# Attention with mixed heads on one Trainium2 core: a head's scores moved in one transfer, and a new order of even and odd steps

## The chip, the cores and the metric

The kernel runs on one core of a Trainium2 chip. The metric is the device time of one execution in microseconds (us). It is the median of several runs. A profile of one further execution shows what each engine and each transfer did.

The engines are named as in the profile: PE (TensorE, matmuls) with PEld (its loads of weights), DVE (VectorE), ACT (ScalarE), POOL (GpSimd) and SP (SyncE). SP does no arithmetic: its queue (SPq) issues nearly all transfers, which 16 DMA engines carry out.

## The reference

Attention whose heads are mixed before and after the softmax, then a feed-forward part with squared ReLU, then a feed-forward part in which each token goes to one of eight experts:

```python
# q, k, v: [4, 12, 448, 64]
scores = scale * q @ k.T                                  # per batch and head: [448, 448]
scores = np.einsum('bhij,hg->bgij', scores, w_pre)        # mix heads
attn = np.exp(scores - max(scores))
attn = attn / (sum(attn) + 1e-9)
attn = np.einsum('bhij,hg->bgij', attn, w_post)           # mix heads again
x = attn @ v                                              # then both feed-forward parts
```

The change is in attention alone.

## The kernel before

Attention works in chunks. A chunk is ten rows of queries with all twelve heads, 120 rows in all, laid over the partitions, so that mixing heads is a matmul over partitions. A batch has 45 chunks (`NCH`), there are four batches, and a step of the main loop in `attention` (variable `g`) finishes one chunk.

*Scores.* `scores(b, t, h)` computes 120 rows (90 for `t` = 3) of one head's scores on PE (L256, L257), copies them from PSUM to a buffer `s` (L260, mostly on ACT; four buffers, `sp`), and sends them with two transfers from SP (L267) into the tile `tt[b, t]`. The transfers put row group `i` of head `h` on partition `12 i + h`: five groups (`HI`) from partition 0 on, the other five from partition 64 on, 60 partitions (`KH`) each. A tile `tt[b, t]` thus gathers twelve heads, and serves twelve chunks (nine for `t` = 3). There are three such tiles in turn.

*Mixing before the softmax.* `pre(b, c)` makes two chunks at a time: four matmuls (L279) of 60 rows by 64 columns of weights `kpre`, each over 448 columns; then the negated maxima on DVE (L292), then two exponentials on ACT (L301) with their sums. `norm` (L310, L311, L313) takes the reciprocal on DVE and scales the second mixing's weights with it on POOL (`kp`).

*Mixing after it.* `post` has four matmuls with `kp` (L323) and moves the result from PSUM to `at` (L331), by ACT for the chunks in `EVAC` and by DVE for the others. `pv` multiplies nine chunks at a time by the values (L344), in two halves; `pv_lo` and `pv_out` split the result in two parts and send it to DRAM (L375).

*Preparation.* `prep` transposes queries and keys of the next batch (L200) and splits them into a high and a low part (L214 on ACT, L233 on DVE); it is a generator in two parts, and a key's high part is copied to the other partitions by SP (L235). `load` (L175) and `load_v` (L243) bring the inputs. For the first batch some of this is done by POOL (L218, L228).

The order is written by hand. `on(g, f, ...)` puts a call into step `g`, with lists such as `PREP` (when a preparation begins) and `EVAC`. Each step has this order:

```python
norm(g + 1)
exp2 = pre(g + 2)      # if that chunk's number is even; exp2 is its second exponential
rest of the step       # scores, prep, pv_lo, pv_out, loads
exp2()
post(g)
pv                     # where one is due
```

Of the kernel before, what the change touches and what calls it, by code (L numbers as in the profile page):

```python
# [19 lines left out]
B, H, S, D = 4, 12, 448, 64  # L20
# [5 lines left out]
II = 10  # L26
NCH = 45
KP = II * H

HI = II // 2  # L30
KH = HI * H
TOKT = 112

TT = 128
# [69 lines left out]
def constants():  # L104

    cols = [n for c in range(NCH) for n in chunk_rows(c)]
    cols = np.array([n for i, n in enumerate(cols) if i not in DUPS])

    orig = np.zeros((128, 3, NTT))
    for t in range(NTT):  # L110
        row = t * TT + np.arange(TT)
        orig[:, 0, t] = (row + 1) // 32 * 32
        orig[:, 1, t] = (row + 1) % 32
        orig[:, 2, t] = row // S * S + cols[row % S]
    orig = orig.reshape(128, -1)
    ident = np.eye(128)
    mask = np.zeros((128, II))
    for i in range(2):
        mask[64 * i:64 * i + KH, HI * i:HI * i + HI] = np.repeat(np.eye(HI), H, axis=0)
    tri = np.triu(np.ones((128, 128)), 1)  # L120
    iota = np.tile(np.arange(128), (128, 1))
    below = np.tile(np.tril(np.ones((NE, NE)), -1).reshape(1, -1), (128, 1))
    im8 = iota[:, :NE] - NE
    return np.concatenate([ident, mask, orig, tri, iota, below, im8], 1).astype(np.float32)

F64_MIN = float(np.array([0x38000000], np.uint32).view(np.float32)[0])
F64_MAX = float(np.array([0x47EFFFFF], np.uint32).view(np.float32)[0])

C_ID, C_MASK, C_ORIG, C_TRI, C_IOTA, C_BELOW, C_IM8 = 0, 128, 138, 180, 308, 436, 500
NCONST = 508


def attention(tc, cst, q, k, v, w_pre, w_post, xscr, nb, tail=None):
    nc = tc.nc
    GC = 9
    NGR = NCH // GC

    def left(name, bufs=1):  # L140
        return Areas(tc, name, bufs)

    wp, at1, vp, xp, mp = left("wp"), left("at1"), left("vp"), left("xp"), left("mp", 3)
    tb, at0, tm, sp, ta = left("tb"), left("at0"), left("tm"), left("sp", 4), left("ta")

    ap_ = (at1, at0) if (NGR * nb - 1) % 2 == 0 else (at0, at1)
    tps = [(tb, ta, tm)[(k + 1 - 4 * nb) % 3] for k in range(3)]
# [10 lines left out]
    ident = cst[:TOKT, C_ID:C_ID + TOKT]  # L158
# [89 lines left out]
    tt = {}  # L248

    def scores(b, t, h):  # L250
        p, j = divmod(h, 2)
        zq = zt[b, p, "q"][0][:, j]
        zkh, zkl = zt[b, p, "k"][0][:, j], zt[b, p, "k"][1]
        n0, m = (120 * t, 120) if t < 3 else (358, 90)
        pq = qk.tile([128, 512], F32, tag="qk", name="pq")
        nc.tensor.matmul(pq[:m, :S], zq[:, n0:n0 + m], zkh, start=True, stop=False)  # L256
        nc.tensor.matmul(pq[:m, :S], zq[:, n0:n0 + m], zkl[:, j], start=False, stop=True)  # L257
        s = sp.tile([120, S], F32, tag="s", name="s")
        eng = nc.vector.tensor_copy if b == t == 0 and h % 3 == 2 else nc.scalar.copy
        eng(s[:m], pq[:m, :S])  # L260
        if h == 0:
            tt[b, t] = tps[(4 * b + t) % 3].tile([128, 12, S], F32, name="t")

        w = m // II
        for j in range(2):
            rows_h = tt[b, t][64 * j:64 * j + KH].rearrange("(i h) r s -> h i r s", h=H)[h]
            nc.sync.dma_start(out=rows_h[:, :w], in_=s[HI * w * j:HI * w * j + HI * w])  # L267

    st = {}

    def pre(b, c):

        t, r = divmod(c, 12)
        single = c == NCH - 1
        pms = [pre_.tile([128, 512], F32, name="pre") for _ in range(2)]
        for i, j in ((0, 0), (1, 1), (0, 1), (1, 0)):
            if single and i != j:
                continue
            nc.tensor.matmul(  # L279
                pms[i][64 * j:64 * j + 64, :S],  # L280
                kpre[64 * i:64 * i + KH],
                tt[b, t][64 * i:64 * i + KH, r if single else r + j],
                start=True,
                stop=True,
            )

        alls = slice(0, 128)
        parts = [(pms[i], halves[i], 0) for i in range(2)] if single else [(pms[i], alls, i) for i in range(2)]
        n = 1 if single else 2
        mxs = [mp.tile([128, 4], F32, tag="mx", bufs=6, name="mx") for _ in range(n)]  # L290
        for pm, q, i in parts:
            nc.vector.tensor_reduce(  # L292
                out=mxs[i][q, 0:1], in_=pm[q, :S], axis=AX.X, op=ALU.max, negate=True
            )
        es = [e_tile() for _ in range(n)]
        for i in range(n):
            st[b, c + i] = [es[i], mxs[i]]

        def exp(k):
            pm, q, i = parts[k]  # L300
            nc.scalar.activation(  # L301
                out=es[i][q], in_=pm[q, :S], func=AF.Exp, bias=mxs[i][q, 0:1], accum_out=mxs[i][q, 1:2]
            )

        exp(0)
        return lambda: exp(1)

    def norm(b, c):
# [97 lines left out]
    tmp = e_tile()  # L406
    wraw = tmp[:, :2 * H].rearrange("p (i h) -> p i h", i=2)
    nc.vector.memset(tmp[:, :2 * H], 0.0)
    for i, w in enumerate((w_pre, w_post)):
        for j in range(2):  # L410
            nc.sync.dma_start(
                out=wraw[64 * j:64 * j + KH, i, :],
                in_=w.rearrange("(o h) g -> o h g", o=1).to_broadcast([HI, H, H]),
            )
    live = [prep(0, *u) for u in units]
    for i in range(len(units) + 3):
        if i < len(units):
# [8 lines left out]
            if LEAD + i - 2 < len(units):  # L426
                load(0, *units[LEAD + i - 2])
    kpre, kpost = (wp.tile([128, n], F32, name=nm) for nm, n in (("kpre", 64), ("kpost", KP)))
    mask = cst[:, C_MASK:C_MASK + II]
    nc.gpsimd.memset(kpre, 0.0)  # L430

    def kron(out, i, q, cols):
        n = cols.stop - cols.start
        nc.gpsimd.tensor_tensor(
            out=out,
            in0=wraw[q, i, :].rearrange("p (h o) -> p h o", o=1).to_broadcast([q.stop - q.start, H, n]),
            in1=mask[q, cols].rearrange("p (o i) -> p o i", o=1).to_broadcast([q.stop - q.start, H, n]),
            op=ALU.mult,
        )

    for j in range(2):
        hq = halves[j]
        kron(kpre[hq, :KH].rearrange("p (i g) -> p g i", i=HI), 0, hq, slice(HI * j, HI * j + HI))
    kron(kpost.rearrange("p (g i) -> p g i", i=II), 1, slice(0, 128), slice(0, II))
    nc.gpsimd.tensor_scalar_mul(kpre, kpre, 1.0 / float(D) ** 0.5)
    chunks = [(b, c) for b in range(nb) for c in range(NCH)]
    at_step = {}
# [1 line left out]
    def on(g, f, *a):  # L449

        rank = 0 if f is go else 2 if f is begin else 1
        at_step.setdefault(g, []).append((rank, f, a))
# [14 lines left out]

    PREP = (14, 15, 17, 19, 20, 22, 24, 25, 27, 29, 31, 32)  # L470
    EVAC = range(15, 34, 3)
    for b in range(nb):
        o = b * NCH
        for h in range(H):
            if b == 0:
                on(-4 + 8 * h // 12, scores, 0, 1, h)
            on(o + (4 if b == 0 else 2) + 10 * h // 12, scores, b, 2, h)
            on(o + 12 + 10 * h // 12, scores, b, 3, h)
            if b + 1 < nb:
                on(o + 26 + 11 * h // 12, scores, b + 1, 0, h)  # L480
                on(o + 37 + 10 * h // 12, scores, b + 1, 1, h)
        for gr in range(NGR):
            end = o + GC * gr + GC
            first, gap = (2, 2) if gr < NGR - 1 and b < nb - 1 else (1, 1)
            if b == nb - 1 and gr == NGR - 1:
                first = 0
            for hf in range(2):
                for i, f in enumerate((pv, pv_lo)):
                    on(end + first + gap * hf + i, f, b, gr, hf)
            on(end + first + gap + 2, pv_out, b, gr)  # L490
        if b + 1 < nb:
            for i, u in enumerate(units):
                spread(o + PREP[i], 2, prep, b + 1, *u)
                on(o + (PREP[i - XB] + 1 if i >= XB else 8 + i), load, b + 1, *u)
        for i in range(4):
            on(o + 3 + 2 * i - 2 * (b == 0), load_v, b, i)

    n = len(chunks)
    last = max(list(at_step) + [n])
    for g in range(-4, last + 1):  # L500
        if 0 <= g + 1 < n:
            norm(*chunks[g + 1])
        exp2 = None
        if 0 <= g + 2 < n and chunks[g + 2][1] % 2 == 0:
            exp2 = pre(*chunks[g + 2])
        rest = [x[1:] for x in sorted(at_step.get(g, []), key=lambda x: x[0])]
        for f, a in rest:
            if f is not pv:
                f(*a)
        if exp2:  # L510
            exp2()
        if 0 <= g < n:
            post(*chunks[g])
        for f, a in rest:
            if f is pv:
                f(*a)
        rel = g - (nb - 1) * NCH
        if rel == 23:
            close(ta, sp, ld, zp, qk)
        if rel == 34:  # L520
            close(tm)
        if rel == 39:
            close(at0)
        if rel == 43:
            close(tb)
        if tail:
            tail(rel)
# [873 lines left out]
```

## Time and profile before

| | |
|---|---|
| time before, median of 3 runs | 1372.76 us (1372.42 to 1373.51) |
| profiled execution, its own time | 1374.09 us |
| its span, first to last instruction | 1372.2 us |
| PE busy | 1282.0 us, 93% of the span |
| DVE busy | 983.3 us, 72% |
| ACT busy | 746.3 us, 54% |
| POOL busy | 162.6 us, 12% |
| mean granted clock of TensorE | 0.978 |

Busy shares are means over stages of different kinds: attention fills the first part of the span, the feed-forward parts the rest. Register, branch and semaphore instructions and the issuing of transfers are not counted as busy. The granted clock is a share of full speed, and has two levels, 1.2 and 2.4 GHz.

### The profile page before, as it was taken

What the parts mean: (1) busy time and instruction counts of PE and PEld (TensorE: products, weight loads), DVE (VectorE), ACT (ScalarE), POOL (GpSimd) and SP (SyncE); (2) the same over time, 40 slices, a digit from 0 to 9 for tenths busy, and PEclk for the clock granted to TensorE, in tenths of its full rate; (3) what the DMA queues carried; (4) which work ended last, traced back from release to release, by engine and by line L of the source; (5) the groups of instructions that cost most, each with busy time, mean ns of one, the idle gap of its engine ahead of it and who ended that gap; (6) DMA issues with size and microseconds to landing.
All of it is one profiled execution on the core that took longest, in us unless ns stands there. A gap on an engine that the chain in (4) does not pass through costs nothing. (4 is left out here: it accounts for less than half of the span.)

```text
span 1372.2 us, 26014 instructions
## 1 busy us (share of the span) xinstructions
PE 1282.0 (93%) x9235; PEld 1116.3 (81%) x9235; DVE 983.3 (72%) x1965; ACT 746.3 (54%) x1469; POOL 162.6 (12%) x249
## 2 busy tenths in 40 slices
PE   6889988998899898999999999999998999999997
PEld 4556666766667676899999999999987899999996
DVE  5447655764676457767986899689647688898887
ACT  5456545654565366454332333333225588889886
POOL 3112221221122122000000000000000111111110
PEclk9899998999999899999999999999999999999999
DMA  5357445645564456756545555446475494556551
GB/s 155 128 150 151 115 132 154 147 118 134 150 142 129 138 120 226 232 184 249 212 189 226 193 227 225 193 176 254 157 263 191 149 361 164 169 179 249 162 179 39
DMA packets 157771, 243.86 MB, mean 178 GB/s; under 512 B 84323, under 2 KB 128707, under 8 KB 149956
## 3 DMA queue, kind: packets, MB, share of 16 engines
q1 hardware_dynamic: 154836, 229.54, 51.6%
q0 software_dynamic: 2800, 12.61, 2.6%
q8 instruction: 75, 1.23, 0.4%
q14 instruction: 60, 0.49, 0.1%
HBM read 236.48 MB, written 23.21 MB: 189 GB/s over the span
## 5 line engine op out<-in xcount | busy, mean ns | idle before, releaser
L323 PEld LDWEIGHTS post_post<-mp_kp,mp_e 128*112 128x112 f32 x1440 | 173.2, 180 | 22.3 <-POOL mp_kp L313 12.5
L323 PE MATMUL post_post<-mp_kp,mp_e 128*112 128x120 f32 x1440 | 181.9, 271 | 6.0 <-POOL mp_kp L313 5.3
L301 ACT ACTIVATE mp_e<-pre_pre,mp_mx 128x448 f32<-128x448 f32 (+1 forms) x184 | 117.1, 637 | 92.3 <-DVE mp_mx L292 91.4
L292 DVE TENSOR_REDUCE mp_mx<-pre_pre 128x1 f32<-128x448 f32 (+1 forms) x184 | 106.4, 618 | 74.0 <-PE pre_pre L279 73.6
L677 PE MATMUL hp_h<-m1x_xl,m1w_ih 128*128 128x384 f32 (+1 forms) x480 | 156.2, 325 | 2.7 <-DMA m1x_xl<-xscrl 2.7
L677 PE MATMUL hp_h<-m1x_xh,m1w_ih 128*128 128x384 f32 (+1 forms) x480 | 156.7, 326 | 0.5 <-DMA m1x_xh<-xscrh 0.5
L260 ACT COPY sp_s<-qk_qk 120x448 f32<-120x448 f32 (+1 forms) x188 | 98.3, 529 | 108.2 <-DMA tb_t<-sp_s 38.4
L686 ACT ACTIVATE m1g_r<-hp_h 128x384 f32<-128x384 f32 (+1 forms) x80 | 37.6, 470 | 218.5 <-PE hp_h L677 205.5
L313 POOL TENSOR_SCALAR mp_kp<-wp_kpost,mp_mx 128x120 f32<-128x120 f32 x180 | 106.3, 592 | 419.7 <-DVE mp_mx L311 355.5
L677 PE MATMUL hp_h<-m1x_xh,m1w_il 128*128 128x384 f32 (+1 forms) x480 | 155.9, 325 | 0.0
L1154 DVE TENSOR_TENSOR m2w_w2l<-m2r_r,m2w_w2h 128x768 fp32r<-128x768 f32 x130 | 116.2, 951 | 33.8 <-ACT m2w_w2h L1153 33.7
L331 DVE COPY at_at<-post_post 112x480 f32<-112x480 f32 x130 | 85.3, 656 | 50.9 <-PE post_post L323 50.1
L770 PE MATMUL acc_a<-m1w_oh,m1g_gl 128*128 128x384 f32 (+1 forms) x436 | 113.2, 341 | 4.1 <-DVE m1g_gl L689 3.9
L770 PE MATMUL acc_a<-m1w_ol,m1g_gh 128*128 128x384 f32 (+1 forms) x436 | 112.3, 339 | 0.0
L770 PE MATMUL acc_a<-m1w_oh,m1g_gh 128*128 128x384 f32 (+1 forms) x436 | 112.1, 338 | 0.0
L784 DVE TENSOR_TENSOR y_y<-acc_a,y_y 128x384 f32<-128x384 f32 x196 | 96.3, 552 | 11.0 <-PE acc_a L770 10.7
L256 PE MATMUL qk_qk<-zp_zk,zp_zq 128*120 128x448 f32 (+1 forms) x192 | 87.1, 453 | 15.5 <-DVE zp_zl L233 5.4
L256 PEld LDWEIGHTS qk_qk<-zp_zk,zp_zq 128*120 128x120 f32 (+1 forms) x192 | 35.0, 182 | 80.5 <-issue 51.5
L1153 ACT CAST m2w_w2h<-m2r_r 128x768 fp32r<-128x768 f32 x130 | 99.0, 841 | 0.3 <-PE m2p_a L1215 0.2
L344 PE MATMUL pv_pv<-at_at,vp_v 112*64 112x90 f32 x1872 | 86.5, 250 | 7.2 <-DMA vp_v<-in_v 6.6
L677 PEld LDWEIGHTS hp_h<-m1x_xl,m1w_ih 128*128 128x128 f32 x480 | 90.5, 189 | 3.2 <-DMA m1x_xl<-xscrl 3.2
L689 DVE TENSOR_TENSOR m1g_gl<-m1g_r,m1g_gh 128x384 fp32r<-128x384 f32 (+1 forms) x78 | 41.1, 528 | 72.2 <-ACT m1g_gh L688 72.2
(239 smaller groups left out, 2697.1 us busy)
## 6 DMA issues: line engine op xcount, KB each, us to landing
m2r_r<-in_moe_w SPq DMA_DIRECT2D x107, 512.0 KB
m2r_r<-in_moe_w SPq DMA_DIRECT2D x136, 384.0 KB
m1x_xh<-xscrh SPq DMA_DIRECT2D x29, 1152.0 KB
m1x_xl<-xscrl SPq DMA_DIRECT2D x29, 1152.0 KB
m1raw_rawi<-in_moe_w_in SPq DMA_DIRECT2D x16, 768.0 KB
m1raw_rawo<-in_moe_w_out SPq DMA_DIRECT2D x16, 768.0 KB
tb_t<-sp_s SPq DMA_DIRECT2D x96, 105.0 KB
ta_t<-sp_s SPq DMA_DIRECT2D x96, 105.0 KB
```

The source lines that it names most:

```text
L256: nc.tensor.matmul(pq[:m, :S], zq[:, n0:n0 + m], zkh, start=True, stop=False)
L260: eng(s[:m], pq[:m, :S])
L292: nc.vector.tensor_reduce(out=mxs[i][q, 0:1], in_=pm[q, :S], axis=AX.X, op=ALU.max, negate=True)
L301: nc.scalar.activation(out=es[i][q], in_=pm[q, :S], func=AF.Exp, bias=mxs[i][q, 0:1], accum_out=mxs[i][q, 1:2])
L313: nc.gpsimd.tensor_scalar_mul(kp, kpost, mx[:, 3:4])
L323: nc.tensor.matmul(po[:, r].rearrange("p g i -> p (g i)"), ev[:, r], kp, start=True, stop=True)
L344: nc.tensor.matmul(px[64 * o:64 * o + 64, p], vt[b][:, g, r], a[:, r, g].rearrange("p c i -> p (c i)"), start=(r == 0), stop=(r == 3),)
L677: nc.tensor.matmul(ph, w[:, k], x, start=(kt == 0 and i == 0), stop=(kt == KT - 1 and i == 2))
L770: nc.tensor.matmul(p, g[:, c], w[:, HM * h:HM * h + (m if h else HM)], start=(j == 0 and i == 0), stop=(j == GF - 1 and i == 2),)
L784: nc.vector.tensor_add(y, p, y)
L1153: nc.scalar.copy(wh, raw)
L1154: nc.vector.tensor_sub(wl, raw, wh.bitcast(F32))
```

## The change

1. A head's scores go in one transfer: ten row groups on partitions `LOW + 12 i + h`, that is 4 to 123, without a gap. The two mixing matmuls now take rows 0 to 63 and 64 to 123. The first four partitions are set to zero once in each of the three tiles, by POOL, and the mixing weights `kpre` are built over 128 partitions with a mask of their own.
2. Five buffers `s` in place of four.
3. In a step the second exponential of the pair before comes first, then the second parts of preparations, then `norm`, the rest, and only then `pre`, `post` and `pv`.
4. Preparations begin in even steps from 14 to 36 of a batch, scores have steps written out (`TILES`), mostly odd ones where preparations run, and `pv` comes in odd steps. `pre` is in even steps, as before.
5. ACT evicts the twelve even chunks from 14 to 36, in place of seven from 15 to 33.
6. The last chunk of a batch, which is a pair of halves, has both exponentials at once.

The core of the diff:

```diff
+LOW = 64 - KH
...
-    tb, at0, tm, sp, ta = left("tb"), left("at0"), left("tm"), left("sp", 4), left("ta")
+    tb, at0, tm, sp, ta = left("tb"), left("at0"), left("tm"), left("sp", 5), left("ta")
...
-        w = m // II
-        for j in range(2):
-            rows_h = tt[b, t][64 * j:64 * j + KH].rearrange("(i h) r s -> h i r s", h=H)[h]
-            nc.sync.dma_start(out=rows_h[:, :w], in_=s[HI * w * j:HI * w * j + HI * w])
+            if 4 * b + t < 3:
+                nc.gpsimd.memset(tt[b, t][:LOW], 0.0)
+
+        rows_h = tt[b, t][LOW:LOW + KP].rearrange("(i h) r s -> h i r s", h=H)[h]
+        nc.sync.dma_start(out=rows_h[:, :m // II], in_=s[:m])
...
-                kpre[64 * i:64 * i + KH],
-                tt[b, t][64 * i:64 * i + KH, r if single else r + j],
+                kpre[64 * i:LOW + KH + KH * i],
+                tt[b, t][64 * i:LOW + KH + KH * i, r if single else r + j],
...
-    PREP = (14, 15, 17, 19, 20, 22, 24, 25, 27, 29, 31, 32)
-    EVAC = range(15, 34, 3)
+    PREP = range(14, 38, 2)
+    EVAC = range(14, 38, 2)
+    TILES = (
+        (25, 25, 27, 27, 29, 31, 33, 33, 35, 37, 39, 39),
+        (35, 37, 38, 40, 41, 41, 42, 43, 43, 44, 45, 46),
+        (2, 3, 3, 4, 5, 6, 7, 8, 9, 10, 11, 12),
+        (13, 13, 15, 15, 17, 17, 19, 19, 21, 21, 23, 23),
+    )
...
-            on(o + (4 if b == 0 else 2) + 10 * h // 12, scores, b, 2, h)
-            on(o + 12 + 10 * h // 12, scores, b, 3, h)
+            on(o + (4 + 9 * h // 12 if b == 0 else TILES[2][h]), scores, b, 2, h)
+            on(o + TILES[3][h], scores, b, 3, h)
             if b + 1 < nb:
-                on(o + 26 + 11 * h // 12, scores, b + 1, 0, h)
-                on(o + 37 + 10 * h // 12, scores, b + 1, 1, h)
+                on(o + TILES[0][h], scores, b + 1, 0, h)
+                on(o + TILES[1][h], scores, b + 1, 1, h)
...
-            first, gap = (2, 2) if gr < NGR - 1 and b < nb - 1 else (1, 1)
+            first, gap = (2 - gr % 2 if gr < NGR - 1 else 1, 2) if b < nb - 1 else (1, 1)
...
+    exp2 = None
     for g in range(-4, last + 1):
+        todo = sorted(at_step.get(g, []), key=lambda x: x[0])
+        rest = [[x[1:] for x in todo if (x[0] == 0) == i] for i in (True, False)]
+        if exp2:
+            exp2()
+        exp2 = None
+        for f, a in rest[0]:
+            f(*a)
         if 0 <= g + 1 < n:
             norm(*chunks[g + 1])
-        exp2 = None
+        for f, a in rest[1]:
+            if f is not pv:
+                f(*a)
         if 0 <= g + 2 < n and chunks[g + 2][1] % 2 == 0:
             exp2 = pre(*chunks[g + 2])
...
-        if exp2:
-            exp2()
         if 0 <= g < n:
             post(*chunks[g])
-        for f, a in rest:
+        for f, a in rest[1]:
             if f is pv:
                 f(*a)
```

## Rows read from the trace of the kernel before

**Rows 1.** Busy time by stretch: stretch, length, engines' busy us (instructions), clock, DMA share, GB/s

```profile
173.80:305.90 132.10, 117.32 (x1167) 87.38 (x1165) 80.31 (x208) 72.36 (x182) 26.18 (x45) 0.95 0.54 137
...
196.60:229.60 33.00, 24.09 (x210) 17.22 (x209) 12.02 (x34) 13.52 (x33) 4.52 (x8) 0.79 0.50 141
229.60:282.10 52.50, 47.02 (x493) 35.34 (x492) 39.01 (x97) 35.73 (x88) 10.94 (x20) 1.00 0.62 144
...
328.70:361.20 32.50, 24.89 (x220) 18.17 (x219) 13.15 (x36) 13.45 (x34) 4.66 (x8) 0.84 0.53 144
...
459.00:486.00 27.00, 21.33 (x185) 15.26 (x184) 9.74 (x27) 9.79 (x25) 3.49 (x6) 0.81 0.37 118
...
44.40:97.00 52.60, 45.06 (x342) 31.51 (x341) 24.95 (x67) 24.63 (x62) 9.04 (x16) 0.94 0.46 137
```

**Rows 2.** Who waited for whom, 60 to 480 us: total us, times, longest us

```profile
ACT sp_s L260 <- DMA tm_t<-sp_s: 30.3, 17, 4.9
ACT sp_s L260 <- DMA tb_t<-sp_s: 30.0, 16, 5.9
...
ACT sp_s L260 <- DMA ta_t<-sp_s: 24.3, 16, 5.2
```

**Rows 3.** Timeline around 200 us: start, us, instruction, idle before it and its releaser

```profile
199.46 0.53 ACT L260 COPY sp_s<-qk_qk 120x448 f32<-120x448 f32 x1 [5.85 <-DMA tb_t<-sp_s]
...
200.67 0.19 PEld L279 LDWEIGHTS pre_pre<-tm_t,wp_kpre 60*64 60x64 f32 x2 [3.81 <-ACT mp_e L301]
```

**Rows 4.** Timeline of SP's queue, 176 to 230 us: start, us, issues

```profile
182.67 4.81 SPq L267 DMA_DIRECT2D tb_t<-sp_s  x6
...
189.52 2.89 SPq L375 DMA_DIRECT2D xscrh<-xp_xh  x1
...
218.55 10.50 SPq L267 DMA_DIRECT2D ta_t<-sp_s  x10
```

**Rows 5.** Issues by line: ns least/median/most, first and last start; then sizes

```profile
L267 SPq DMA_DIRECT2D ta_t<-sp_s x120: 712/727/2912, 33.1 to 443.5; - x120
...
L235 SPq DMA_DIRECT2D zp_zk<-zp_zk x36: 512/545/1859, 99.7 to 409.6; - x36
...
L175 SPq DMA_DIRECT2D ld_x<-in_q x18: 642/650/1702, 72.2 to 385.6; - x18
...
L375 SPq DMA_DIRECT2D xscrh<-xp_xh x28: 519/610/2892, 97.5 to 565.7; - x28
...
tb_t<-sp_s SPq DMA_DIRECT2D x96, 105.0 KB
```

**Rows 6.** Busy time while SP issues scores only (columns as in rows 1)

```profile
182.70:187.40 4.70, 4.70 (x69) 3.67 (x66) 2.49 (x8) 1.92 (x5) 0.79 (x2) 1.00 0.33 120
```

**Rows 7.** Timeline of one chain from mixing to the next weights

```profile
233.16 0.98 PE L279 MATMUL pre_pre<-tm_t,wp_kpre 60*64 60x448 f32 x8
...
234.19 1.16 DVE L292 TENSOR_REDUCE mp_mx<-pre_pre 128x1 f32<-128x448 f32 x2
...
234.85 0.63 ACT L301 ACTIVATE mp_e<-pre_pre,mp_mx 128x448 f32<-128x448 f32 x1 [1.26 <-DVE mp_mx L292]
...
235.38 1.26 DVE L233 TENSOR_TENSOR zp_zq<-qk_qk,zp_zq 64x448 fp32r<-64x448 f32 x2
...
236.67 0.15 DVE L310 TENSOR_SCALAR mp_mx<-mp_mx 128x1 f32<-128x1 f32 x1
...
237.29 0.58 POOL L313 TENSOR_SCALAR mp_kp<-wp_kpost,mp_mx 128x120 f32<-128x120 f32 x1 [2.26 <-DVE mp_mx L311]
```

**Rows 8.** Groups by line: busy us, mean ns of one, idle before

```profile
L331 DVE COPY at_at<-post_post 112x480 f32<-112x480 f32 x130 | 85.3, 656 | 50.9 <-PE post_post L323 50.1
...
L331 ACT COPY at_at<-post_post 112x480 f32<-112x480 f32 x50 | 27.9, 571 | 2.4 <-PE post_post L323 2.2
```

**Rows 9.** The first 40 us: POOL's zeroing, and the first mixing

```profile
L228 POOL MEMSET zp_zl<- x12: 464/466/467, 9.3 to 24.6; 64x448 f32 x12
...
37.01 2.55 PE L279 MATMUL pre_pre<-tb_t,wp_kpre 60*64 60x448 f32 x8 [5.31 <-DMA tb_t<-sp_s]
```

More of the change, by code (lines that the diff above doesn't have):

```diff
@@ L119, in constants @@
         mask[64 * i:64 * i + KH, HI * i:HI * i + HI] = np.repeat(np.eye(HI), H, axis=0)
+    rmask = np.zeros((128, HI))
+    for j in (LOW, 64):
+        rmask[j:j + KH] = np.repeat(np.eye(HI), H, axis=0)
     tri = np.triu(np.ones((128, 128)), 1)
@@ L123, in constants @@
     im8 = iota[:, :NE] - NE
-    return np.concatenate([ident, mask, orig, tri, iota, below, im8], 1).astype(np.float32)
+    return np.concatenate([ident, mask, orig, tri, iota, below, im8, rmask], 1).astype(np.float32)
 F64_MIN = float(np.array([0x38000000], np.uint32).view(np.float32)[0])
 F64_MAX = float(np.array([0x47EFFFFF], np.uint32).view(np.float32)[0])
-C_ID, C_MASK, C_ORIG, C_TRI, C_IOTA, C_BELOW, C_IM8 = 0, 128, 138, 180, 308, 436, 500
-NCONST = 508
+C_ID, C_MASK, C_ORIG, C_TRI, C_IOTA, C_BELOW, C_IM8, C_RMASK = 0, 128, 138, 180, 308, 436, 500, 508
+NCONST = 513
 def attention(tc, cst, q, k, v, w_pre, w_post, xscr, nb, tail=None):
@@ L305, in pre @@
         exp(0)
+        if single:
+            exp(1)
+            return None
         return lambda: exp(1)
@@ L408, in attention @@
     nc.vector.memset(tmp[:, :2 * H], 0.0)
[L409 to L414, printed above, removed]
+    for i, w, q0, n in ((0, w_pre, LOW, II), (1, w_post, 0, HI), (1, w_post, 64, HI)):
+        nc.sync.dma_start(
+            out=wraw[q0:q0 + n * H, i, :],
+            in_=w.rearrange("(o h) g -> o h g", o=1).to_broadcast([n, H, H]),
+        )
     live = [prep(0, *u) for u in units]
@@ L428, in attention @@
     kpre, kpost = (wp.tile([128, n], F32, name=nm) for nm, n in (("kpre", 64), ("kpost", KP)))
-    mask = cst[:, C_MASK:C_MASK + II]
     nc.gpsimd.memset(kpre, 0.0)
-    def kron(out, i, q, cols):
-        n = cols.stop - cols.start
+    for i, out, m in (
+        (0, kpre[:, :KH].rearrange("p (i g) -> p g i", i=HI), cst[:, C_RMASK:C_RMASK + HI]),
+        (1, kpost.rearrange("p (g i) -> p g i", i=II), cst[:, C_MASK:C_MASK + II]),
+    ):
+        n = m.shape[1]
         nc.gpsimd.tensor_tensor(
             out=out,
-            in0=wraw[q, i, :].rearrange("p (h o) -> p h o", o=1).to_broadcast([q.stop - q.start, H, n]),
-            in1=mask[q, cols].rearrange("p (o i) -> p o i", o=1).to_broadcast([q.stop - q.start, H, n]),
+            in0=wraw[:, i, :].rearrange("p (h o) -> p h o", o=1).to_broadcast([128, H, n]),
+            in1=m.rearrange("p (o i) -> p o i", o=1).to_broadcast([128, H, n]),
             op=ALU.mult,
         )
[L441 to L444, printed above, removed]
     nc.gpsimd.tensor_scalar_mul(kpre, kpre, 1.0 / float(D) ** 0.5)
@@ L466, in spread @@
             on(g + i, go, (f, a))
-    PREP = (14, 15, 17, 19, 20, 22, 24, 25, 27, 29, 31, 32)
-    EVAC = range(15, 34, 3)
+    PREP = range(14, 38, 2)
+    EVAC = range(14, 38, 2)
+    TILES = (
[4 rows of a table added]
+    )
     for b in range(nb):
@@ L499, in attention @@
     last = max(list(at_step) + [n])
+    exp2 = None
     for g in range(-4, last + 1):
+        todo = sorted(at_step.get(g, []), key=lambda x: x[0])
[5 more added lines that the diff above has]
+            f(*a)
         if 0 <= g + 1 < n:
             norm(*chunks[g + 1])
-        exp2 = None
+        for f, a in rest[1]:
+            if f is not pv:
+                f(*a)
         if 0 <= g + 2 < n and chunks[g + 2][1] % 2 == 0:
             exp2 = pre(*chunks[g + 2])
-        rest = [x[1:] for x in sorted(at_step.get(g, []), key=lambda x: x[0])]
-        for f, a in rest:
-            if f is not pv:
-                f(*a)
-        if exp2:
-            exp2()
         if 0 <= g < n:
             post(*chunks[g])
-        for f, a in rest:
+        for f, a in rest[1]:
             if f is pv:
```

## The prediction

> **What bounds the kernel now.** Attention fills the first 545 us or so of the span; the two feed-forward parts behind it keep TensorE filled, and nothing in them changes, so what attention gains or loses goes to the end one for one. I first cut attention into stretches by the view of busy time per window [rows 1]. One batch period (45 chunks, 48 heads of scores) lasts 132.1 us, of which TensorE is busy for 117.32 at a mean granted clock of 0.95. The loss is not spread evenly. Between 196.6 and 229.6 us TensorE is busy for 24.09 of 33.0 us at a clock of 0.79; directly behind it, where the next batch's queries and keys are also transposed, it is busy for 47.02 of 52.5 at 1.00. The same hole stands in the next two batches, at 328.7 (32.5 us) and 459.0 (27.0 us).
>
> The two levels of the clock are 1.2 and 2.4 GHz, so a mean of 0.79 is 42% of the stretch at the lower one. That level is a consequence: it stands where TensorE had just been idle. What a hole costs is its idle time plus half the busy time at the lower level: 8.9 + 33.0 x 0.42 x 0.73 / 2 = 14.0 us; by the same working 11.6 us for the one at 328.7 and 9.7 us for that at 459.0. The first 53 us of chunks (44.4 to 97.0) lose 7.5 + 2.7 = 10.2 us [rows 1].
>
> Next I asked who waits for whom. In 60 to 480 us ScalarE's copies of scores out of PSUM wait for 84.6 us (30.3 + 30.0 + 24.3) for a transfer of scores to land, because their four buffers are all in flight [rows 2]. ScalarE runs in order, so the exponentials behind such a copy wait too: at 199.46 a copy starts after 5.85 us of idleness, and TensorE's mixing at 200.67 had then stood 3.81 us for the exponential [rows 3]. That is how a late transfer becomes an idle TensorE.
>
> Then the question why transfers are late. SyncE's queue shows issues end to end: six in 4.81 us, then, once there is a backlog, one of the output's issues at 2.89 us and ten issues of scores in 10.50 us [rows 4]. An issue of scores takes 0.727 us at the median and 2.9 at most; a copy of 64 keys 0.545, a load of queries 0.650 [rows 5]. Between 182.7 and 187.4, where the queue issues scores only, the DMA engines are busy at 0.33 of 16, moving 120 GB/s [rows 6]: 5.3 engines at work. A transfer of scores writes 5 partitions (`HI`), which fits with five engines each taking one. At 120 GB/s, 105 KB last 0.90 us, so a head's two last 1.8 us, and 48 heads (12 of them of 90 rows, three quarters as long) 81 us of the 132, ahead of what the other transfers put on the same engines. So both the queue (2 x 0.727 us a head) and the few engines are close to what a step of 2.9 us offers, and every burst makes a hole.
>
> **The change, part by part.** *One transfer in place of two.* 192 of 384 issues go. The new one moves 210 KB into 10 partitions. Its issue is not in the trace: between 0.51 (the shortest copy of a key) and twice 0.727; I take 0.73, since issues of very different size lie between 0.55 and 0.73 at the median [rows 5]. Its duration: 0.90 us if ten engines work on it as five did, 1.8 if still five. I take 0.90, because the share in rows 6 follows the partitions written. A head then asks 0.9 us of its engines and 0.73 of the queue, half of before, and a fifth buffer adds to that. The queue's other issues stay, but gather in odd steps: two copies of a key, a load, two pieces of output and two heads are 2 x 0.545 + 0.65 + 2 x 0.61 + 2 x 0.73 = 4.4 us [rows 5], against 5.2 us for two steps; behind a late one stand the other issues, and ScalarE's copies only once five buffers are out. At twice 0.727 it would be 5.9 us, and the odd steps would be the queue's.
>
> What ten partitions get, the row can't say. The Trainium skill, "DMA: Bandwidth & Descriptors", section "Why a DMA increments its semaphore by 16 and not by 1", gives a rule that would make them five now and ten then: the number of engines is the largest up to 16 that divides the slowest dimension of both sides. By it the duration is 0.9 us, as taken above.
>
> What returns: the holes should fill as well as the stretch that runs beside the transposes does now, 47.02/52.5 = 0.90. 33.0 us then become (33.0 - 14.0)/0.90 = 21.1, a gain of 11.9; 32.5 become 23.2 (9.3); 27.0 become 19.2 (7.8); 52.6 become 47.1 (5.5). Sum 34.5 us. At 0.97 it would be 42; if only half returned, 17.
>
> *The order of a step.* Even steps now have mixing, transposes and ScalarE's eviction, odd steps two heads of scores, the second half of the preparation and the values' product. All engines but TensorE have room: in the 52.5 us beside the transposes VectorE is busy 39.01 and ScalarE 35.73 us [rows 1]. What I expect is fewer waits of TensorE for a buffer that a transpose or score still holds: fill 0.95 in place of 0.90 there, 52.5 to 49.5, 3.0 us in each of three batches, 9 us. Bounds: 0 to 12 (fill 0.97).
>
> *Maxima later.* The chain from mixing to the next weights now begins behind the scores or transposes of its step. In the trace it takes from 233.16 to 237.87, 4.7 us: maximum at 234.19, exponential 234.85, sum 236.67, weights 237.29 for 0.58 [rows 7]. VectorE's subtractions already lie inside it. The product that needs the weights comes two steps later, behind a mixing of 0.98: 2 x 2.6 + 0.98 = 6.2 us. 1.5 us are left, so I put it at nothing. The second exponential moves to the head of the next step; its product is one step later still.
>
> *Sixteen evictions* move from VectorE (0.656 us) to ScalarE (0.571) [rows 8]: 10.5 us less on the one, 9.1 more on the other, hidden under TensorE; if ScalarE had no room, 9.1 us. *Sixty-four rows in place of sixty* in half of the mixing matmuls: 448 columns stay, so nothing; at most 0.98 x 4/60 in 90 pairs, 6 us.
>
> *The start.* Zeroing four partitions of 12 x 448 is not in the trace; by the 0.466 us for 448 on GpSimd [rows 9] it takes 5.6 us, three times. The second falls before any weights are due; behind the third the weights of the next step queue, which have a step of 2.6 to spare: at most 3 us, and I take nothing. The first stands ahead of the zeroing of a key's low part and delays head 2. Against that the first mixing, which now waits 5.31 us for the last of 24 transfers [rows 9], waits for 12. Between 5.31 - 5.6 = -0.3 and 5.3; I take 2.5. Fewer loads of the mixing weights and one product less there are covered by the same wait.
>
> Sum: 34.5 + 9 + 2.5 = 46 us. The profiled execution took 1374.09 us (span 1372.2), 1.3 above the median of 1372.76, so 1374.1 - 46 - 1.3 = 1326.8, told as 1327.
>
> **The rivals.** *Transfers stay as long (chance 0.10).* If the merged transfer lasts 1.8 us on five engines, or if both halves already used the same engines, only issues are saved. The engines' load of a head is as before and holes remain; the fifth buffer and the new order give perhaps the 9 us, and 1374.1 - 9 - 1.3 = 1364. For it: the queue too is full in the holes. Against it: 0.33 busy with issues end to end [rows 6]. The Trainium skill, "DMA: Bandwidth & Descriptors", section "Rules for kernel authors", says that transfers to two halves of the partitions both spread over all 16 engines; that would be this case, and the 0.33 speaks against it.
>
> *Gains are taken back (0.04).* Freed holes run into the next limit, the in-order queues of ScalarE with more evictions and copies in the same step: 1372 plus or minus 2.
>
> *The later maxima become the wait (0.06), slower.* If the chain grows to more than two steps of 2.9 plus 0.98, 6.9 us, TensorE stands for weights in every pair. It takes 2.2 us more in VectorE's queue ahead of the sum: both subtractions (1.26) and an eviction (0.66) would nearly do. At 7.4 us a pair is 0.5 longer; 22.5 pairs in 3 batches make 34 us, less the 15 that the transfers still return in the start and the last batch: 1392. Against it: the subtractions are in the 4.7 already.
>
> **How the numbers follow.** The forecast, 0.80, has its own range of 1299 (all losses counted above, 45.5 in the holes, 5.5 in each of three stretches of preparation and 5.3 at the start, 67 us, and a tenth more, since a busy TensorE is not one at its peak) to 1350 (half the sum). The whole range, 1298 to 1352, leaves out the three rivals, 0.20. Less than 0.2% (2.7 us) is no change that a measurement of this kernel can tell. Faster: 0.80 + 0.10 and a little of the fourth, 0.91; same 0.03; slower 0.06.
>
> **What would show it.** In the profile after: 192 issues of scores at 0.6 to 0.9 us; where only scores are issued, a DMA share above 0.5 for as long as they are in flight; ScalarE's copies waiting for landings under 20 us in place of 84.6; no stretch with a clock below 0.9 after the first mixing; a batch period near 118 us. The prediction is wrong if landings stay on five engines' pace, if TensorE's waits for the weights (GpSimd's line) become its largest, or if the first mixing comes after 37.0 us.

## The result, and the profile after

The changed kernel takes 1303.11 us (median of 4 runs, 1300.77 to 1306.98), beside 1373.13 us for the kernel before (4 runs, 1372.42 to 1375.70): a ratio of 0.949 [0.946, 0.952], 70 us faster. The forecast was 1327 us. The time lies in the range and the direction is right; the gain was put at 46 us and is half as large again. The profiled execution took 1304.41 us with a span of 1302.6.

The page of the changed kernel, its busy times and the row of the granted clock in 40 slices of 32.6 us:

```profile
PE 1256.1 (96%) x9235; PEld 1100.4 (84%) x9235; DVE 973.8 (75%) x1949; ACT 751.8 (58%) x1485; POOL 176.6 (14%) x251
...
PEclk8899999999998999999999999999999999999999
```

TensorE is busy for 96% of the span. Only three slices of the clock stand below 9 (0.9 or more): the two of the start and the thirteenth, which holds 391 to 423 us.

Busy time by stretch of the changed kernel (columns as in [rows 1]); the first two are one batch period each, and the last two are a stretch in which SyncE issues scores only, and a hole that is left:

```profile
148.70:262.20 113.50, 110.42 (x1160) 83.11 (x1159) 76.68 (x202) 73.50 (x186) 26.32 (x45) 0.98 0.68 158
262.20:374.00 111.80, 110.03 (x1167) 82.85 (x1166) 77.52 (x204) 73.86 (x186) 26.33 (x45) 1.00 0.71 163
...
31.70:38.00 6.30, 2.74 (x12) 0.88 (x12) 0.16 (x1) 2.13 (x4) 1.12 (x1) 0.77 0.63 210
402.00:416.00 14.00, 11.08 (x105) 8.29 (x102) 3.80 (x10) 4.25 (x12) 1.20 (x3) 0.76 0.34 95
```

A batch period that took 132.1 us [rows 1] takes 113.5 and 111.8. TensorE is busy for 97% and 98% of it, where it was 89%. The holes of [rows 1] are gone; one is left in the last batch, at 402 us, and it has another cause (below). Where only scores move, the DMA share is 0.63 of 16, or 10.1 engines, at 210 GB/s; it was 0.33 and 120 GB/s [rows 6].

The waits of ScalarE's copies for landings, by buffer, in 60 to 480 us of the changed kernel (columns: total us, times, longest):

```profile
ACT sp_s L266 <- DMA tb_t<-sp_s: 2.3, 3, 1.1
...
ACT sp_s L266 <- DMA tm_t<-sp_s: 1.0, 2, 0.7
...
ACT sp_s L266 <- DMA ta_t<-sp_s: 0.4, 1, 0.4
```

That is 3.7 us in place of 84.6 [rows 2]. Attention's last product of values starts at 495.2 us after and at 561.9 before, by the two traces' instructions of that line: 66.7 of the 69.7 us between the two profiled executions arose in attention, as the prediction assumed.

### The profile page after: what moved, and what is told of

Read it like the earlier page. It is cut to its first block, busy times and chain, and to the rows that moved or that the text cites. A ratio compares the mean times of both kernels' runs of the same rounds, so it can differ in the third digit from the quotient of the medians.

```text
span 1302.6 us, 25715 instructions
## 1 busy us (share of the span) xinstructions
PE 1256.1 (96%) x9235; PEld 1100.4 (84%) x9235; DVE 973.8 (75%) x1949; ACT 751.8 (58%) x1485; POOL 176.6 (14%) x251
## 5 line engine op out<-in xcount | busy, mean ns | idle before, releaser
L332 PEld LDWEIGHTS post_post<-mp_kp,mp_e 128*112 128x112 f32 x1440 | 165.9, 177 | 73.9 <-issue 37.6
L332 PE MATMUL post_post<-mp_kp,mp_e 128*112 128x120 f32 x1440 | 185.1, 272 | 2.8 <-POOL mp_kp L322 2.8
L266 ACT COPY sp_s<-qk_qk 120x448 f32<-120x448 f32 (+1 forms) x188 | 94.5, 536 | 23.5 <-PE qk_qk L263 12.5
L799 DVE TENSOR_TENSOR y_y<-acc_a,y_y 128x384 f32<-128x384 f32 x196 | 96.3, 552 | 11.0 <-PE acc_a L785 10.7
L692 PEld LDWEIGHTS hp_h<-m1x_xh,m1w_ih 128*128 128x128 f32 x480 | 90.1, 188 | 0.3
L692 PEld LDWEIGHTS hp_h<-m1x_xh,m1w_il 128*128 128x128 f32 x480 | 90.1, 188 | 0.0
L340 DVE COPY at_at<-post_post 112x480 f32<-112x480 f32 x114 | 74.6, 655 | 18.8 <-PE post_post L332 17.7
```

The lines of the kernel that those rows point to most:

```text
L332: nc.tensor.matmul(po[:, r].rearrange("p g i -> p (g i)"), ev[:, r], kp, start=True, stop=True)
L340: eng(at[b, gr][:, :, :, cc, :], po)
L692: nc.tensor.matmul(ph, w[:, k], x, start=(kt == 0 and i == 0), stop=(kt == KT - 1 and i == 2))
L799: nc.vector.tensor_add(y, p, y)
```

## The experiments

Each edit is against the changed kernel, except where the text says otherwise. Experiments 1 to 4, 5 to 7 and 8 to 11 are three groups of runs, each on a chip of its own, with the kernel before beside them at 1373.92, 1372.91 and 1374.07 us. The changed kernel took 1303.11 us in the runs of the section above and 1300.00 in the third group, so a difference between groups is uncertain by some 3 us.

**1. The transfer alone.** The changed kernel with the old order within a step, the old lists of which chunk gets which work, and four buffers: of the change only the merged transfer is left, with what it needs (partitions 0 to 3 zeroed, the mixing weights laid out to fit).

> The old kernel with the one transfer per head alone: four buffers, the old order of a step and the old lists. Theory of the prediction (late transfers make the holes): most of the 70 us come, 1310 to 1335 us, and ScalarE's waits for landings of scores (84.6 us in 60 to 480 before) fall below 20 us. Rival (the even and odd order does it): 1355 to 1370 us. Rival (both are needed): 1335 to 1355 us.

Measured: 1326.57 us (1323.31 to 1330.47), ratio 0.967 [0.964, 0.969]: 47 us of the 70. The waits for landings, in the same view as above, and the stretch where the first hole had been:

```profile
ACT sp_s L266 <- DMA tb_t<-sp_s: 8.9, 5, 3.9
ACT sp_s L266 <- DMA ta_t<-sp_s: 7.6, 8, 3.2
ACT sp_s L266 <- DMA tm_t<-sp_s: 7.4, 5, 3.7
```

```profile
200.00:220.00 20.00, 18.61 (x213) 13.98 (x206) 16.03 (x41) 15.43 (x37) 4.66 (x8) 1.00 0.73 177
```

The waits are 23.9 us (under 20 had been expected), and the hole has filled to 18.61/20.0 = 0.93 at a clock of 1.00 (0.79 in [rows 1]).

**2. All but the transfer.** The changed kernel with two transfers of five partitions each, as before.

```
-        rows_h = tt[b, t][LOW:LOW + KP]...[h]
+        w = m // II
+        for j in range(2):
+            rows_h = tt[b, t][LOW + KH * j:LOW + KH * j + KH]...[h]
+            nc.sync.dma_start(out=rows_h[:, :w], in_=s[HI * w * j:HI * w * j + HI * w])
-        nc.sync.dma_start(out=rows_h[:, :m // II], in_=s[:m])
```

> The changed kernel with a head's scores again in two transfers of five row groups, written to the new partitions; new order, new lists, five buffers. Theory of late transfers: 1345 to 1370 us, the holes near 0.8 clock are back, a lone stretch of scores shows a DMA share near 0.33. Rival (the order does it): 1303 to 1320 us. Rival (both are needed): 1325 to 1345 us.

Measured: 1364.33 us (1361.04 to 1370.15), ratio 0.993 [0.991, 0.995]. The new order, the lists and the fifth buffer, with transfers as they were, give 10 us. The first row is a stretch in which SyncE issues scores only: the DMA share is 0.33 again. The packets of the trace show what that is: five are under way at once for 76% of this stretch, and never fewer. In the changed kernel's stretch of scores alone (31.9 to 37.0 us) ten are under way for 56% of the time, and never fewer than eight. The other two rows are holes, which are back in other places:

```profile
36.00:50.00 14.00, 10.78 (x60) 6.19 (x60) 5.28 (x16) 6.63 (x16) 2.31 (x4) 0.71 0.33 122
...
200.00:216.00 16.00, 8.60 (x95) 6.76 (x91) 3.51 (x12) 3.85 (x10) 2.09 (x4) 0.75 0.62 157
320.00:340.00 20.00, 12.04 (x122) 9.07 (x117) 6.49 (x20) 6.05 (x15) 3.31 (x6) 0.85 0.64 165
```

TensorE now stands in them for another transfer than in [rows 3]: for loads of values, which the same queue issues late (9.3 and 8.0 us in 195 to 220 and 315 to 342 us). In 60 to 480 us its two largest waits are

```profile
PE pv_pv L355 <- DMA vp_v<-in_v: 24.0, 7, 6.6
PE qk_qk L262 <- DMA zp_zk<-zp_zk: 12.3, 7, 3.1
```

that is, for values and for copies of keys; in the changed kernel they are 5.6 and 0.3 us.

So 47 us alone and 10 us alone make 70 together. The 13 us that are over belong to both: the order (with the lists and the buffer) is worth 10 us where transfers are late and 23 us (1326.57 to 1303.11) where they are not.

**3. Ten partitions, but two issues.** Two transfers again, each with half the columns of all ten partitions. The bytes are the same, cut into pieces of 896 bytes in place of 1,792.

```
-        nc.sync.dma_start(out=rows_h[:, :m // II], in_=s[:m])
+        for j in range(2):
+            c = slice(S // 2 * j, S // 2 * j + S // 2)
+            nc.sync.dma_start(out=rows_h[:, :m // II, c], in_=s[:m, c])
```

> The changed kernel with two transfers per head as well, but cut by columns: each writes 224 of the 448 columns into all ten partitions, so the count of issues is doubled as in the run of two transfers by rows, and the partitions written by each are ten. If the number of DMA engines per transfer is what counts: 1303 to 1318 us. If the queue's issues are what counts: as the run of two transfers by rows, 1340 to 1370 us.

Measured: 1331.83 us (1327.07 to 1333.68), ratio 0.969 [0.966, 0.972]. Both expectations missed: it lies between the two. Of the 61 us between experiment 2 and the changed kernel, 32 come back with ten partitions to a transfer, and the other 29 only with one issue in place of two. SyncE's issues of scores, in this kernel (L275) and then in the changed one (L273); columns: count, ns least/median/most, first and last start:

```profile
L275 SPq DMA_DIRECT2D tb_t<-sp_s x144: 755/756/1844, 12.8 to 466.3; - x144
```

```profile
L273 SPq DMA_DIRECT2D tb_t<-sp_s x72: 755/756/2545, 11.8 to 439.6; - x72
```

An issue to ten partitions costs 0.756 us whether it moves 105 or 210 KB. From the timeline of SyncE's queue in 150 to 260 us I added up the issues one by one: 130 issues take 96.0 of 110 us in experiment 3, 87 take 69.6 in the changed kernel (121 and 94.6 in experiment 2, 118 and 92.5 before). Between two issues that follow each other the queue pauses for some 0.05 to 0.1 us, so 130 issues leave it next to no room, however fast the engines are. What that looks like in experiment 3 (start, duration; a row of several issues includes the pauses between them):

```profile
200.78 7.66 SPq L275 DMA_DIRECT2D ta_t<-sp_s  x8
208.49 0.59 SPq L386 DMA_DIRECT2D xscrh<-xp_xh  x1
209.18 0.60 SPq L386 DMA_DIRECT2D xscrl<-xp_xl  x1
...
212.35 3.39 SPq L275 DMA_DIRECT2D ta_t<-sp_s  x4
```

Each row starts within 0.1 us of the end of the one above it, the two left out too. What waits behind such a queue are the other transfers. In 60 to 480 us TensorE stands 10.7 us for loads of values and, longest of all, for copies of keys:

```profile
PE qk_qk L262 <- DMA zp_zk<-zp_zk: 11.8, 5, 5.3
```

The smaller pieces may have a part in the 29 us. In a stretch where SyncE issues scores only, end to end, the row is

```profile
36.00:50.00 14.00, 12.53 (x81) 7.98 (x82) 7.48 (x22) 7.86 (x21) 2.94 (x6) 0.80 0.46 127
```

A piece of 896 bytes takes an engine 41 ns at the median of this stretch, where one of 1,792 takes 74 in the changed kernel, so the same bytes cost the engines a tenth more. But the share of 0.46 is below the 0.63 that ten partitions reached there, so in this stretch the queue sets the pace. No run separates the pieces from the second issue over the whole kernel.

**4. Four buffers.** `left("sp", 5)` becomes `left("sp", 4)`.

> The changed kernel with four buffers of scores in place of five. Theory: once a transfer lasts 0.9 us the fifth buffer is worth little, 1302 to 1308 us. Rival (the fifth buffer carries the bursts): 1312 us or more, with ScalarE waiting for landings again.

Measured: 1299.06 us (1295.26 to 1305.51), ratio 0.945 [0.942, 0.948]. The fifth buffer is worth nothing once a head is one transfer. ScalarE's waits for landings come back all the same, 26.2 us (11.1 + 9.7 + 5.4) in place of 3.7, and cost nothing that can be measured. Their sum alone therefore doesn't say what a late landing costs; it counts where TensorE then stands.

**5. The old lists.** `PREP`, `EVAC` and the steps of the scores and of the values' product as before; the new order within a step.

> The changed kernel with the old lists of steps (preparations, scores, values' products, ScalarE's evictions where they were), and the new order within a step. The run of the transfer alone took 1326.6 us, the whole change 1303.1, so the order is worth some 23 us beside the merged transfer. Theory: the lists give it (an even step never holds scores, an odd one never the mixing), so 1318 to 1328 us here. Rival: the order within a step gives it, 1303 to 1312 us.

Measured: 1321.64 us (1319.87 to 1322.17), ratio 0.962 [0.960, 0.965]: 19 us slower than the changed kernel at 1303.11.

**6. The old order within a step.** The loop over the steps as before; the new lists.

> The changed kernel with the old order within a step (mixing first, second exponential behind the scores) and the new lists. Theory that the lists give the 23 us: 1303 to 1312 us. Rival that the order within a step gives them: 1318 to 1328 us. If each alone gives nothing and only both together do, both this run and the one with the old lists are near 1325 us.

Measured: 1312.98 us (1309.80 to 1313.43), ratio 0.955 [0.953, 0.958]: 10 us slower than the changed kernel, between the ranges of the two theories.

**7. The maxima's place alone.** Only the mixing and its maxima go back ahead of the step's scores and transposes. The second exponential stays at the head of the step after.

```
+        if 0 <= g + 2 < n and chunks[g + 2][1] % 2 == 0:
+            exp2 = pre(*chunks[g + 2])
         for f, a in rest[1]:
             if f is not pv:
                 f(*a)
-        if 0 <= g + 2 < n and chunks[g + 2][1] % 2 == 0:
-            exp2 = pre(*chunks[g + 2])
```

> The changed kernel with the mixing and its maxima ahead of a step's scores and transposes again; the second exponential still at the head of the next step, the lists new. Theory of the prediction (the later maxima cost and bring nothing by themselves): 1300 to 1308 us. Rival (the later place brings the gain, since TensorE no longer stands for the exponential of two steps before): 1312 us or more. Rival (the later place costs): below 1298 us.

Measured: 1320.30 us (1319.48 to 1324.68), ratio 0.962 [0.959, 0.965]: 17 us slower than the changed kernel. The theory of the prediction missed, and the rival that the later place brings a gain holds. The groups of mixing in 60 to 480 us, first of this kernel, then of the changed one (columns: count, busy us, mean ns, idle before and its releaser):

```profile
L285 PE MATMUL pre_pre<-tm_t,wp_kpre 64*64 64x448 f32 (+1 forms) x228 | 37.9, 573 | 0.5
L285 PE MATMUL pre_pre<-ta_t,wp_kpre 64*64 64x448 f32 (+1 forms) x228 | 36.1, 574 | 1.0 <-ACT mp_e L307 0.7
L285 PE MATMUL pre_pre<-tb_t,wp_kpre 64*64 64x448 f32 (+1 forms) x200 | 34.3, 561 | 1.9 <-ACT mp_e L307 1.6
```

```profile
L285 PE MATMUL pre_pre<-tm_t,wp_kpre 64*64 64x448 f32 (+1 forms) x228 | 32.0, 569 | 0.0
L285 PE MATMUL pre_pre<-tb_t,wp_kpre 64*64 64x448 f32 (+1 forms) x212 | 30.0, 562 | 1.6 <-ACT mp_e L307 1.6
L285 PE MATMUL pre_pre<-ta_t,wp_kpre 64*64 64x448 f32 (+1 forms) x228 | 29.8, 576 | 0.0
```

Matmuls that follow each other freely overlap, eight of 0.57 us in 0.98; a wait between them spreads them out, and the group counts as busy for longer. 37.9 + 36.1 + 34.3 = 108.3 us against 32.0 + 30.0 + 29.8 = 91.8: matmuls of the same mean length, and no more of them, stretch over 16.5 us more, as much as the loss. Where it sits is seen in the timeline of experiment 7 (start, duration, releaser in brackets), a pair of weight loads and matmuls with the exponential between:

```profile
223.53 2.09 PE L285 MATMUL pre_pre<-tb_t,wp_kpre 64*64 64x448 f32 x8
223.87 0.63 ACT L307 ACTIVATE mp_e<-pre_pre,mp_mx 128x448 f32<-128x448 f32 x1
...
224.64 0.20 PEld L285 LDWEIGHTS pre_pre<-tb_t,wp_kpre 60*64 60x64 f32 x6 [0.92 <-ACT mp_e L307]
```

and the same pair in the changed kernel:

```profile
211.90 0.21 ACT L307 ACTIVATION_READ_ACCUMULATOR mp_e<-pre_pre,mp_mx 128x1 f32 x1
212.07 0.39 PEld L206 LDWEIGHTS qk_qk<-cst_cst,ld_x 112*128 112x128 f32 x4
...
212.61 0.98 PE L285 MATMUL pre_pre<-tb_t,wp_kpre 64*64 64x448 f32 x8
```

Mixing writes two PSUM tiles a pair. At the head of its step the second of them is still being read by the second exponential of the pair before, and TensorE stands in mid-mixing: 2.09 us for what takes 0.98. With the transposes ahead of it, the exponential has ended at 212.11, before mixing begins. Experiment 6 has the same wait, a smaller one, since there the second exponential runs in its own step, ahead of the next mixing. Its groups, and one such wait in its timeline, read

```profile
L285 PE MATMUL pre_pre<-tm_t,wp_kpre 64*64 64x448 f32 (+1 forms) x228 | 35.0, 576 | 0.2 <-ACT mp_e L307 0.2
L285 PE MATMUL pre_pre<-ta_t,wp_kpre 64*64 64x448 f32 (+1 forms) x228 | 34.6, 576 | 0.5 <-ACT mp_e L307 0.4
L285 PE MATMUL pre_pre<-tb_t,wp_kpre 64*64 64x448 f32 (+1 forms) x204 | 31.5, 562 | 0.2 <-ACT mp_e L307 0.2
```

```profile
221.25 0.20 PEld L285 LDWEIGHTS pre_pre<-tb_t,wp_kpre 60*64 60x64 f32 x6 [0.65 <-ACT mp_e L307]
```

35.0 + 34.6 + 31.5 = 101.1 us, 9.3 more than the changed kernel has: nearly all of the 10 us that experiment 6 loses. The 17 us of experiment 7 are the price of a mixed order that neither kernel has.

**8. The first zeroing at the very start.** GpSimd zeroes the first tile's four partitions ahead of all its other work in attention (at 0.75 us).

```
-            tt[b, t] = tps[(4 * b + t) % 3].tile([128, 12, S], F32, name="t")
-            if 4 * b + t < 3:
+            if 4 * b + t:
+                tt[b, t] = tps[(4 * b + t) % 3].tile([128, 12, S], F32, name="t")
+            if 0 < 4 * b + t < 3:
...
+    tt[0, 0] = tps[0].tile([128, 12, S], F32, name="t")
+    nc.gpsimd.memset(tt[0, 0][:LOW], 0.0)
     LEAD = 12
```

> The changed kernel with the first tile's four partitions zeroed at the very start, when GpSimd has nothing to do, in place of ahead of the second key's low part. In the changed kernel TensorE waits 4.07 us for that low part. Theory (the zeroing of 4.57 us is on the path of the start): 3 to 5 us faster than the changed kernel, 1298 to 1301. Rival (the start is held by the transfers of the first tile anyway): no change, 1302 to 1304.

Measured: 1296.36 us (1295.42 to 1298.68), ratio 0.944 [0.941, 0.947], beside 1300.00 us for the changed kernel on the same chip (experiment 11).

**9. Values loaded earlier.** In batches after the first, the four loads of values go to steps 2, 3, 4 and 5 in place of 3, 5, 7 and 9.

```
-            on(o + 3 + 2 * i - 2 * (b == 0), load_v, b, i)
+            on(o + (1 + 2 * i if b == 0 else 2 + i), load_v, b, i)
```

> The changed kernel with the four loads of values in steps 2, 3, 4 and 5 of a batch in place of 3, 5, 7 and 9 (first batch as before). In the changed kernel the last one is issued at 399.85 and its product waits until 407.9, with a clock of 0.83 in that stretch. Theory (this is what is left of the holes): 5 to 10 us faster than the changed kernel, 1293 to 1298. Rival (the transfers in front of it only move): 1301 to 1305.

Measured: 1290.43 us (1289.10 to 1291.85), ratio 0.940 [0.936, 0.943], 10 us below experiment 11. It answers to the hole at 402 us that the changed kernel kept. A load of values on SyncE's queue, and the product on TensorE, in the changed kernel's timeline:

```profile
399.85 0.33 SPq L249 DMA_DIRECT2D vp_v<-in_v  x1
...
407.94 2.66 PE L353 MATMUL pv_pv<-at_at,vp_v 112*64 112x90 f32 x30 [2.92 <-DMA vp_v<-in_v]
```

The last load of values is issued at 399.85, and the product that needs it starts 8 us later, after 2.92 us of idleness; the mean clock of the stretch is 0.76. With the loads earlier no wait for values is left in 60 to 480 us, and the busy time of the same place is

```profile
380.00:410.00 30.00, 30.00 (x300) 21.65 (x292) 19.27 (x56) 17.87 (x48) 7.84 (x14) 1.00 0.63 166
```

**10. Both.** Experiments 8 and 9 together.

> The changed kernel with both: the first zeroing at the very start and the values' loads earlier. If both theories hold: 1289 to 1294 us, faster than both kernels. If neither: 1301 to 1305.

Measured: 1284.99 us (1284.17 to 1286.40), ratio 0.936 [0.932, 0.939]: it beats both kernels, the changed one by 15 us. Two batch periods of it:

```profile
145.90:255.80 109.90, 109.37 (x1168) 82.71 (x1170) 77.67 (x204) 73.83 (x187) 26.36 (x46) 1.00 0.70 164
255.80:366.30 110.50, 109.73 (x1168) 82.63 (x1168) 77.50 (x204) 73.82 (x187) 26.26 (x46) 1.00 0.69 166
```

TensorE is busy for 99.5% and 99.3% of them at full clock: in these stretches waits leave next to nothing to gain.

**11. The changed kernel once more**, for the comparison on one chip.

> The changed kernel itself on the same chip as the three runs with an earlier zeroing and earlier loads, as their measure: 1300 to 1307 us.

Measured: 1300.00 us (1295.48 to 1301.81), ratio 0.946 [0.942, 0.949]. The ranges of experiments 8 to 10 were reckoned from some 1303 us, and all three runs came out below them. Counted from 1300.00 they gain 3.6, 9.6 and 15.0 us: the first two as their theories say (3 to 5, and 5 to 10), the third a little more than the 9 to 14 that its range means.

## Why the prediction was right, and where its sizes were off

**What bounds the kernel: right.** Late transfers made the holes. With the merged transfer alone (experiment 1) the waits for landings fall from 84.6 us [rows 2] to 23.9, and 47 of 70 us are gained. Of the 24 us that the forecast missed, some 10 belong to the transfer and 14 to the order.

**One transfer: right, its size low.** An issue was taken at 0.73 us and measures 0.756. The duration was taken as that of ten engines, and the DMA share of 0.63 and the packets under way say ten. The first rival, that a transfer would stay as long (1364 us), fell with it. That experiment 2 came out at 1364.33 is chance: it has two issues a head, where the rival had one. It is chance too that the transfer alone, at 1326.57, lies on the forecast for the whole change.

The mis-sized term is how far the holes refill: I took 0.90, the fill beside the transposes. Experiment 1 has 0.93 where the first hole had been, and the changed kernel 0.97 to 0.98 over whole batch periods. The term was 34.5 us ("at 0.97 it would be 42"); with the start's 2.5 it makes 37 beside the 47 of experiment 1. At 0.93 the four holes make 38 by the same working, so some 7 us of the 47 lie outside of them. The stretch beside the transposes was a poor ceiling because another wait held it. In its 52.5 us (229.6 to 282.1 of the kernel before) ScalarE waits 0.8 us for landings, and TensorE waits 5.4 us, 4.7 of them for VectorE's splits:

```profile
PE qk_qk L256 <- DVE zp_zl L233: 1.9, 2, 1.1
PE qk_qk L200 <- DVE zp_zq L233: 1.5, 2, 0.8
```

The Trainium skill, "DMA: Bandwidth & Descriptors", section "Why a DMA increments its semaphore by 16 and not by 1", would give five engines before and ten after; 0.33 and 0.63 of 16 agree. The Trainium skill, in the same page's section "Rules for kernel authors", advises against two transfers to two halves of the partitions, because both would share all 16 engines anyway. The advice fits what was gained here. The reason doesn't hold for transfers of five partitions: issued end to end and alone, they have five packets under way and a share of 0.33 (experiment 2).

**The queue: half seen.** The prediction named the queue as close to its limit and halved its issues, but priced engines and queue as one hole. Experiment 3 parts them: 32 us for the engines, 29 for the issue (with the smaller pieces).

**The order of a step: the step that failed.** It was put at 9 us with 12 as the most; experiment 1 against the changed kernel has 23. The part that was expected came, and larger: TensorE's waits for a buffer that VectorE's splits still hold are 12.9 us in 60 to 480 us of experiment 1 (4.5 + 4.4 + 2.2 + 1.8) and none in the changed kernel, where the prediction priced a fill of 0.95 in place of 0.90. Its parts:

- *Maxima later* was "1.5 us are left, so I put it at nothing". That sum looked at the chain from mixing to the weights, and whether it would come late. For the matmuls it didn't: those with the new weights wait 1.2 us in 60 to 480 us, and the rival of 1392 us falls. What the sum left out is the other side of the same move: mixing writes a PSUM tile that the last exponential still reads. Beside the new lists the order within a step is worth 10 us (experiment 6), and 9.3 of them are that wait.
- *The lists* are worth 19 us (experiment 5). In 60 to 480 us of that kernel two of TensorE's groups read

```profile
L332 PE MATMUL post_post<-mp_kp,mp_e 128*112 128x120 f32 x1288 | 166.5, 273 | 7.2 <-POOL mp_kp L322 7.2
...
L206 PE MATMUL qk_qk<-cst_cst,ld_x 112*128 112x112 f32 x144 | 20.1, 261 | 2.6 <-ACT sp_s L266 2.1 <-DVE zp_zq L239 0.5
```

  and in the changed kernel

```profile
L332 PE MATMUL post_post<-mp_kp,mp_e 128*112 128x120 f32 x1343 | 172.8, 272 | 1.2 <-POOL mp_kp L322 1.2
...
L206 PE MATMUL qk_qk<-cst_cst,ld_x 112*128 112x112 f32 x144 | 21.6, 273 | 0.0
```

  That is 6.0 us for the weights and 2.6 for buffers of transposes; the second is what the prediction expected in kind. All of TensorE's waits in that view come to 21.8 us against 11.3. The other 8 of the 19 us are not accounted for.
- These parts don't add: 19 us for the lists and 10 for the order within a step taken back one at a time, 23 together (with the fifth buffer).

**Left at nothing, and nothing:** the fifth buffer (experiment 4), and 64 rows in mixing: its median is 587 ns before, and 587, 587 and 572 by tile after. The 16 evictions were tried only with the lists.

**The start: off by 1.5.** Zeroing was estimated at 5.6 us and takes 4.57. The rows of the changed kernel's start:

```profile
10.74 4.57 POOL L270 MEMSET tb_t<- 4x5376 f32 x1
15.34 0.99 POOL L234 MEMSET zp_zl<- 64x448 f32 x2
15.87 0.28 PEld L263 LDWEIGHTS qk_qk<-zp_zl,zp_zq 128*120 128x120 f32 x1 [4.35 <-POOL zp_zl L234]
...
36.03 1.77 PE L285 MATMUL pre_pre<-tb_t,wp_kpre 64*64 64x448 f32 x8 [3.02 <-DMA ta_t<-sp_s]
```

The zeroing of a key's low part queues behind it, and TensorE's load of weights stands 4.35 us for it, as described; the first mixing comes at 36.03 in place of 37.01 [rows 9], so 1.0 us and not 2.5. In experiment 8 it comes at 30.35. At the end that is 3.6 us in medians with intervals that overlap; on top of experiment 9 it is 5.4 us (1290.43 to 1284.99), with runs that don't overlap.

**The signs.** 192 issues near 0.76 us, the share above 0.5, the waits under 20 us and the first mixing before 37.0 came as said. The batch period came out shorter (113.5 and 111.8, not 118). The clock didn't come as said: its mean is 0.76 in the hole at 402 us. The wait for values that makes it stands in the kernel before too (inside the hole of [rows 1] that begins at 459.0):

```profile
476.39 1.46 PE L344 MATMUL pv_pv<-at_at,vp_v 112*64 112x90 f32 x30 [1.90 <-DMA vp_v<-in_v]
```

The prediction had put that hole down to scores alone. One sign of being wrong came by one reading, that TensorE's waits for GpSimd's line become its largest. In the changed kernel its loads of weights for the second mixing have that as their largest wait on another engine:

```profile
PEld post_post L332 <- POOL mp_kp L322: 28.4, 39, 1.1
```

It did little harm: the matmuls behind these loads stood 1.2 us in all, and TensorE was busy for 97 to 98% of a batch period.

## What to carry to other kernels

Count a transfer twice, as an issue on its queue and as so many partitions on the DMA engines; where both are near their limit, merging two transfers frees both. Here the partitions gave 32 of 61 us, and the issue, with the size of the pieces, 29. When an instruction is moved, look not only at who waits for its result but also at who still reads the buffer that it writes. When a large hole closes, price a better order afresh: it was worth 10 us beside late transfers and 23 without them. And take the fill that a hole will reach from a stretch with the same limit: the one taken here was held by another wait.

## What the runs showed of the hardware

- An issue on SyncE's queue takes the same 0.756 us for 105 KB (experiment 3) and 210 KB (changed kernel), so twice the bytes to ten partitions cost the queue nothing more.
- A transfer's DMA share followed the partitions written: 5.3 of 16 engines for five ([rows 6] and experiment 2), 10.1 for ten (changed kernel), with mostly five and ten packets under way at once. Where the queue set the pace, ten partitions had 7.4 (0.46, experiment 3).
- Issues follow each other on the queue with 0.05 to 0.1 us between them (experiment 3).
- GpSimd's zeroing of 4 partitions by 5,376 takes 4.57 us, 0.85 ns an element, less than the 0.466 us for 448 [rows 9] gives (1.04).
